# A fused sliding-window attention and channel mix: v in rows of two tokens, batch 0 by plain loads, bias products apart, new instruction orders

## The chip, the cores and the metric

One Trainium2 chip, of which the kernel uses one core. The time of a run is the device time of one launch in microseconds (us). Engines: TensorE (PE), VectorE (DVE), ScalarE (ACT), GpSimd (POOL) and SyncE (SP); in this kernel POOL and SP issue the DMA transfers.

## The reference

q, k and v are of the shape (8, 8, 576, 64), that is batch, heads, tokens, head size, in fp32. The attention has a sliding window of 128 tokens and an ALiBi bias; its result is the input of a channel mix.

```python
scores = (1.0 / np.sqrt(D)) * np.matmul(q, k.transpose(0, 1, 3, 2))
rel = pos[:, None] - pos[None, :]
slopes = 2.0 ** (-8.0 * (np.arange(H) + 1) / H)
bias = slopes[:, None, None] * (-np.abs(rel))[None]
mask = (rel >= 0) & (rel < 128)
attn = softmax(np.where(mask, scores + bias[None], -1e9))
x = np.matmul(attn, v)                     # (8, 8, 576, 64)
x = x.transpose(0, 2, 1, 3).reshape(8, 576, 512)
x_prev = x moved by one token, zeros first
xk = mu_k * x + (1.0 - mu_k) * x_prev
xr = mu_r * x + (1.0 - mu_r) * x_prev
k = np.maximum(xk @ w_k, 0.0)              # w_k 512 x 1024
out = 1.0 / (1.0 + np.exp(-(xr @ w_r))) * (k * k @ w_v)   # fp32, (8, 576, 512)
```

## The kernel before

The attention is cut into 32 items: item 4b + g is batch b with the head pair g (heads 2g and 2g + 1). The 576 tokens are four blocks of 128 and a tail of 64. Scores are made with keys on the partitions and queries along the free axis, so that the next product needs no transpose of them; of each block of keys only the 256 queries that can see it are computed, in two halves (`HALVES`) of 2 x 512 columns.

An item goes through these steps (in brackets the names of the steps in the order tables, then the tiles in the trace):

- Loads. v by POOL, cast to bf16 on the way, a block of 128 tokens at a time (lvs.b.j, tile vs; lvs.b.4 is the tail, tile tv). The vs and tv rows hold a column of ones beside each head, so that the product with v also gives the sum of the softmax. q and k of batches 1 to 4 by POOL, also cast, four tokens of a head to a partition row (lql, tile ql); batches 5 to 7 a block of tokens at a time (lqn, into the same tile) and then transposed by DMA from SP (tr, tile qt). The q and k of each batch's tail are loaded by POOL (lts, tile ts) and transposed on PE (tail, copied to tile tt by tcopy), or for batches 5 to 7 by DMA from SP (trt).
- In batches 0 to 4: a copy that puts tokens in order (ct on DVE, tile ct), transposes on PE (tq and tk, tile tp, line 166), copies out of PSUM (pq and pk, tile qk, line 146). For head pair 0 of batch 0, q and k come as fp32 by SP (lq, tile qt) and are cast by DVE (c, line 143).
- Scores (score.item.half, tile sa, line 229). Items 0 to 3 (`EARLY`) add the ALiBi bias and the mask on PE: a product of a scaled identity (sid) with a table of distances (dist) is summed into the same PSUM tile, line 206, in the same step. All later items instead multiply by a table after the exp.
- exp (exp, ACT, line 237, tile at), then that product by the table (mask, DVE, line 246; not for items 0 to 3).
- The product with v (av, PE, line 262), the division (norm, DVE, tile xu), the transpose to channels on the partitions (ot on PE and xt on ACT, or for items 12 and later a DMA transpose xt from SP), and the token shift (xk and xr, DVE; the tile dl is x minus its predecessor).

Pairs P of batches share one channel mix. Its columns are cut into chunks starting at c0: m1 (PE, line 326, w_k) gives one of 8 groups of 128 features, rl is its relu (ACT, line 332), kk the square (DVE line 341, or ACT line 338), m3 (PE, line 349, w_r) and rs (ACT tanh, line 355) the gate, m2a and m2 (PE, line 364, w_v) the two halves of the second product, oo its product with the gate (DVE, line 379), st the store (SP).

What runs when is written out by hand: a table `ORDER` gives for each engine the names of all its steps in a row, and `plan()` emits them in that order; each engine works through its row and waits where an input or a buffer isn't free. PSUM has two buffers for sa and four for everything else (mm). Before PE has anything to do it runs warm-up products on a zero tile (line 190; tile wm): eight written out, then `FILL` = (5, 2, 3).

Of the kernel before, what the change touches and what calls it, by code (L numbers as in the profile page):

```python
# [16 lines left out]
def kernel(  # L17
# [26 lines left out]
    W = D + 1  # L44
    NBUF = 4
# [31 lines left out]
    ldr = qt_buf[-1].rearrange("p i j g c -> p (i j g c)").bitcast(FP32)[  # L77
        :, 0:4 * NHW * NF * D].rearrange("p (i g h c) -> p i g h c", i=2, g=NHW, h=2)
# [32 lines left out]
    def load_qk(g, i):  # L111
        nc.sync.dma_start(
            out=ldr[:, i, g],
            in_=(q, k)[i][0, 2 * g:2 * g + 2, 0:SM].rearrange("h (p r) d -> p h (r d)", p=128))

    def load_v(b, j):
        if j < NF:
            nc.gpsimd.dma_start(  # L118
                out=vs_buf[b % NLD][:, j, :, 0:D],
                in_=v[b, :, 128 * j:128 * j + 128, :].rearrange("h p d -> p h d"))  # L120
        else:
            nc.gpsimd.dma_start(
                out=tv_buf[b % NLD][0:64, :, 0:D],
                in_=v[b, :, SM:S, :].rearrange("h p d -> p h d"))

    def load_qp(g, i):
        nc.gpsimd.dma_start(
            out=ql_buf[0][:, g // 2, i, 2 * (g % 2):2 * (g % 2) + 2],
            in_=(q, k)[i][0, 2 * g:2 * g + 2, 0:SM].rearrange("h (p r) d -> p h (r d)", p=128))
# [32 lines left out]
    def qk_transp(it, t0, t1):  # L162
        cs = T["cs", it]
# [19 lines left out]
    def tail_copy(b):  # L183
        t4 = T.pop(("tt", b))[:, 0:128 * G].rearrange("p (g t c) -> p g t c", g=G, t=2)
        nc.vector.tensor_copy(out=tt_buf[b % 2][:, :, 0:3:2], in_=t4)

    def warm(n):
        ps = p_mm.tile([128, 512], FP32, tag="mm", name="wm")
        for _ in range(n):
            nc.tensor.matmul(ps, lhsT=zero[:, 0:128], rhs=zero, start=True, stop=True)  # L190

    BASE = (0, 256, 512, 768, 960)
    HALVES = (((0, 0, 256), (1, 128, 256)),
              ((2, 256, 256), (3, 384, 128), (3, 512, 64), (4, 512, 64)))

    def scores(it, e):
# [4 lines left out]
        a0 = BASE[pieces[0][0]] + pieces[0][1] - 128 * pieces[0][0]  # L201
        w = sum(n for _, _, n in pieces)
        sa = T["sa", it, e] = p_sa.tile([128, 2, 512], FP32, tag="sa", name="sa")
        if early:
            for hl in range(2):
                nc.tensor.matmul(
                    sa[:, hl, 0:w] if e else sa[:, hl, 0:w].rearrange("p (u c) -> p u c", u=2),
                    lhsT=sid[:, 2 * g + hl],
                    rhs=dist if e else dist[:, None, 0:256].to_broadcast([128, 2, 256]),
                    start=True, stop=False, skip_group_check=True)  # L210
# [21 lines left out]
    def at_half(it, e):  # L232
        return at_buf[it % NAT][:, 0:2048].rearrange(
# [797 lines left out]
```

## Time and profile before

| what | value |
|---|---|
| runs | 231.13, 231.31, 230.84 us; median 231.13 us |
| profiled execution | span 230.5 us, 5326 instructions |
| PE matmul busy | 222.2 us, 96% of the span |
| DVE busy | 192.2 us, 83% |
| ACT busy | 155.4 us, 67% |
| POOL busy | 88.7 us, 38% |
| DMA | 33.56 MB read, 9.44 MB written, mean 146 GB/s of 16 engines' payload |

The span runs from the first to the last instruction of the profiled execution. Busy time of POOL and SP does not count the issue of a DMA as such; the lines of the trace named DMA_DIRECT2D on POOL are the work that POOL does to make a transfer's descriptors. In a line of the stretches, "10.00, 8.89 (x119)" after the window is its length, then busy time and instructions of PE, and so on for each engine in the order of the head line. In a line in order of time the first number is the start, the second the busy time of the group, and the bracket tells the idle time of the engine before it and what ended that. In a line of groups the bar separates names from busy time and mean (ns), and the last part is the idle time ahead of that group.

### The profile page before, as it was taken

The numbers are of one execution on the slowest core, as the hardware profiler recorded it, in microseconds if no ns is written. First come the engines' busy times: TensorE is split into PE (matmuls) and PEld (weight loads), VectorE is DVE, ScalarE is ACT, GpSimd is POOL, SyncE is SP. The second block draws the span as 40 slices with busy tenths as digits, with TensorE's granted clock in tenths as the row PEclk, the third lists the DMA queues.
The fourth block names the chain that finished last, engine by engine and source line by source line (L and its number), as shares of the span: only waits on it lengthen the run. The fifth ranks groups of instructions, "written<-read, shape, count | busy, mean of one in ns | idle before, by whom it ended". The sixth has DMA issues, their size and how long they took to land.

```text
span 230.5 us, 5326 instructions
## 1 busy us (share of the span) xinstructions
PE 222.2 (96%) x2099; PEld 130.0 (56%) x2099; DVE 192.2 (83%) x409; ACT 155.4 (67%) x265; POOL 88.7 (38%) x127
## 2 busy tenths in 40 slices
PE   7889899999999999999999999899999999999994
PEld 2446577855685565456657554455574555456653
DVE  7577999999998998999798996996876998985252
ACT  4299999985999998783789555685168744226700
POOL 8987857563897000697001954540000000000000
PEclk9999999999999999999999999999999999999999
DMA  6999999999999986999996999999954252413014
GB/s 137 160 173 187 198 177 192 195 180 162 177 155 161 154 120 100 123 128 204 120 256 144 166 120 156 203 176 197 134 128 119 79 163 77 102 46 141 0 67 162
DMA packets 117305, 33.65 MB, mean 146 GB/s; under 512 B 99608, under 2 KB 112928, under 8 KB 117280
## 3 DMA queue, kind: packets, MB, share of 16 engines
q0 software_dynamic: 83600, 16.52, 92.3%
q1 hardware_dynamic: 33680, 16.79, 34.1%
q8 instruction: 16, 0.26, 0.4%
q14 instruction: 9, 0.07, 0.1%
HBM read 33.56 MB, written 9.44 MB: 187 GB/s over the span
## 4 chain that ended last, share of the span: by engine, by line
PE 84%; ACT 7%; DMA 4%; DVE 2%; issue 1%; SPq 0%; DVEq 0%
PE pv L364 25%; PE ps L326 25%; PE pr L349 13%; PE sa L262 7%; PE sa L229 6%; DMA tt<-ts 4%; PE wm L190 3%; PE tp L166 3%; ACT at L237 3%; ACT qk L146 2%; PE pv L371 2%; ACT xt L287 1%; PE tp L282 1%; DVE qk L143 1%; ACT rl L332 1%
## 5 line engine op out<-in xcount | busy, mean ns | idle before, releaser
L237 ACT ACTIVATE at<-sa 128x1024 bf16<-128x1024 f32 x64 | 64.7, 1043 | 14.3 <-PE sa L229 14.2
L326 PE MATMUL ps<-xk,wk_sb 128*128 128x256 bf16 (+2 forms) x416 | 73.2, 314 | 0.5 <-DVE xk L315 0.4
L332 ACT ACTIVATE rl<-ps 128x256 bf16<-128x256 f32 (+2 forms) x104 | 46.3, 482 | 37.0 <-PE ps L326 30.0
L364 PE MATMUL pv<-wv_sb,kk 128*128 128x512 bf16 x272 | 65.3, 379 | 0.0
L326 PEld LDWEIGHTS <-wk_sb 128*128 128x128 bf16 x416 | 38.5, 98 | 24.1 <-issue 2.4
L364 PEld LDWEIGHTS <-kk 128*128 128x128 bf16 x272 | 25.5, 98 | 28.4 <-issue 1.3
L246 DVE TENSOR_TENSOR at<-at,mask 128x1024 bf16<-128x1024 bf16 x56 | 37.4, 684 | 1.9 <-ACT at L237 1.9
L118 POOL DMA_DIRECT2D vs<-in_v_dram x32 | 28.5, 897 | 26.3 <-PE sa L262 16.1
L341 DVE TENSOR_TENSOR kk<-rl 128x256 bf16<-128x256 bf16 (+2 forms) x88 | 28.0, 335 | 10.3 <-ACT rl L332 10.1
L349 PE MATMUL pr<-wr_sb,xr 128*128 128x512 bf16 x144 | 36.0, 379 | 0.0
L379 DVE SCALAR_TENSOR_TENSOR ot<-rs,pv 128x512 f32<-128x512 bf16 (+1 forms) x38 | 24.4, 653 | 7.4 <-PE pv L364 5.8
L315 DVE SCALAR_TENSOR_TENSOR xk<-dl,mu_sb,xt 128x576 bf16<-128x576 bf16 (+2 forms) x36 | 27.1, 752 | 1.3
L315 DVE SCALAR_TENSOR_TENSOR xr<-dl,mu_sb,xt 128x576 bf16<-128x576 bf16 x32 | 25.5, 812 | 0.0
L355 ACT ACTIVATE rs<-pr 128x512 bf16<-128x512 f32 x36 | 21.5, 608 | 4.9 <-PE pr L349 4.6
L262 PEld LDWEIGHTS <-at 128*128 128x128 bf16 x576 | 21.6, 98 | 5.3 <-issue 0.4
L274 DVE TENSOR_TENSOR xu<-sa,rc 128x640 bf16<-128x640 f32 x28 | 23.1, 824 | 1.2 <-DMA xt<-xu 0.3
L146 ACT COPY qk<-tp 128x1024 bf16<-128x1024 bf16 (+1 forms) x20 | 18.9, 960 | 5.6 <-PE tp L166 4.6
L349 PEld LDWEIGHTS <-xr 128*128 128x128 bf16 x144 | 13.2, 98 | 12.6 <-issue 0.4
L90 POOL DMA_DIRECT2D ql<-in_k_dram x12 | 10.9, 919 | 23.0 <-DVE ct L157 21.1
L262 PE MATMUL sa<-vs,at 128*128 128x65 bf16 x448 | 18.9, 194 | 0.0
L308 DVE TENSOR_TENSOR dl<-xt 128x576 bf16<-128x576 bf16 (+2 forms) x36 | 15.1, 420 | 3.2 <-DMA xt<-xu 2.1
L229 PE MATMUL sa<-qk 64*128 64x256 bf16 (+1 forms) x160 | 13.2, 259 | 0.8 <-ACT qk L146 0.5
(70 smaller groups left out, 207.6 us busy)
## 6 DMA issues: line engine op xcount, KB each, us to landing
out_dram<-ot SPq DMA_DIRECT2D x34, 256.0 KB, 3.6
vs<-in_v_dram POOLq DMA_DIRECT2D x32, 128.0 KB, 8.0
ql<-in_k_dram POOLq DMA_DIRECT2D x9, 256.0 KB, 6.7
ql<-in_q_dram POOLq DMA_DIRECT2D x9, 256.0 KB, 7.3
ql<-in_k_dram POOLq DMA_DIRECT2D x13, 128.0 KB, 6.5
ql<-in_q_dram POOLq DMA_DIRECT2D x13, 128.0 KB, 7.6
wk_sb<-in_moe_w_k_dram POOLq DMA_DIRECT2D x2, 512.0 KB, 9.0
wv_sb<-in_moe_w_v_dram POOLq DMA_DIRECT2D x2, 512.0 KB, 8.5
```

The lines of the kernel that those rows point to most:

```text
L118: nc.gpsimd.dma_start(out=vs_buf[b % NLD][:, j, :, 0:D], in_=v[b, :, 128 * j:128 * j + 128, :].rearrange("h p d -> p h d"))
L229: nc.tensor.matmul(to, lhsT=kk_, rhs=qq_, start=not early, stop=True, skip_group_check=True)
L237: nc.scalar.activation(out=at_half(it, e), in_=T.pop(("sa", it, e)), func=AF.Exp, scale=float(scale))
L246: nc.vector.tensor_tensor(out=at, in0=at, in1=m, op=ALU.mult)
L262: nc.tensor.matmul(pa[:, hl, W * (t - t0):W * (t - t0) + W], lhsT=at[:, lo:lo + 128], rhs=vs[:, u, 2 * g + hl, :] if u < NF else tvb[:, 2 ...
L315: nc.vector.scalar_tensor_tensor(out=to, in0=T["dl", it][:, c0:c1], scalar=mu_sb[:, NPO * which + g:NPO * which + g + 1], in1=xp, op0=ALU. ...
L326: nc.tensor.matmul(ps[:, 0:c1 - c0], lhsT=wk_sb[:, po, 128 * fo:128 * fo + 128], rhs=xk[:, po, c0:c1], start=(po == 0), stop=(po == NPO - 1))
L332: nc.scalar.activation(out=rl[:, 0:c1 - c0], in_=T.pop(("ps", P, c0, fo))[:, 0:c1 - c0], func=AF.Relu, scale=RELU_SCALE)
L341: nc.vector.tensor_tensor(out=T["kk", P, c0][:, fo, 0:c1 - c0], in0=rl[:, 0:c1 - c0], in1=rl[:, 0:c1 - c0], op=ALU.mult)
L349: nc.tensor.matmul(pr, lhsT=T["xr", P][:, po, 128 * c:128 * c + 128], rhs=wr_sb[:, po], start=(po == 0), stop=(po == NPO - 1))
L364: nc.tensor.matmul(pv, lhsT=kk[:, fo, o:o + 128], rhs=wv_sb[:, fo], start=(fo == 0), stop=(fo == NFO - 1))
L379: nc.vector.scalar_tensor_tensor(out=T["ot", P, c][:, w0:w1], in0=T["rs", P, c][:, w0:w1], scalar=1.0, in1=pv[:, 0:w1 - w0], op0=ALU.add, ...
```

## The change

What it does, part by part:

- *v.* `load_v` fetches rows of two tokens (2 x 64 numbers of a head) into partitions 0 to 63; a new step vc.b.z moves the odd tokens of two blocks to partitions 64 to 127, one copy for two blocks. On the partitions a block's tokens are then the 64 even ones and the 64 odd ones. k is brought into the same order: pk permutes in its copy, the lqn loads of k come in two halves of 64 partitions (36 loads for three batches, where there were 24), and dist and the mask are made for that order. The column of ones stands ahead of a head's numbers.
- *Batch 0.* All four head pairs come as fp32 through SP (8 loads, 2 before) into the two qt buffers, and are cast by steps c.g.i on three engines (2 on DVE, 4 on ACT, 2 on POOL) into the memory of ql; the four POOL loads of batch 0's q and k are gone, as are its three ct steps.
- *Bias.* The products with dist are steps of their own, bias.item.half, which can stand well ahead of the scores that add to them.
- *q and k copies.* pq and pk are steps of 512 columns each, for every item up to 19.
- *Tables.* dist and mask are 320 wide, not 512, and the copies that filled the rest (dcopy, mcopy) are gone; zero, dist, sid and the row of mu lie in the memory of w_v, so that the load of w_v waits for their last use.
- *Warm-ups.* `FILL` goes from (5, 2, 3) to (2, 2): 18 products become 12.
- *Squares.* 46 of 104 on ACT, where 16 were; 58 on DVE, where 88 were.
- *Other copies.* 4 of 16 xt copies go from ACT to DVE, two tcopy steps from DVE to ACT. 6 vc steps are on DVE, 10 on POOL. The ring of rs has 5 buffers instead of 6.
- *Orders.* All memsets stand ahead of POOL's first load, and all five tables are new.

The core of the diff:

```diff
-    vs_buf = [cst.tile([128, NF, H, W], BF16, name=f"vs{i}") for i in range(NLD)]
+    vs_buf = [cst.tile([128, NF, H, V0 + 2 * D], BF16, name=f"vs{i}") for i in range(NLD)]
...
     def load_v(b, j):
         if j < NF:
             nc.gpsimd.dma_start(
-                out=vs_buf[b % NLD][:, j, :, 0:D],
-                in_=v[b, :, 128 * j:128 * j + 128, :].rearrange("h p d -> p h d"))
+                out=vs_buf[b % NLD][0:64, j, :, V0:],
+                in_=v[b, :, 128 * j:128 * j + 128, :].rearrange("h (p r) d -> p h (r d)", r=2))
...
+    def v_copy(b, j, f):
+        vs = vs_buf[b % NLD][:, 2 * j:2 * j + 2].rearrange("p j h c -> p (j h) c")
+        f(vs[64:128, :, V0:V0 + D], vs[0:64, :, V0 + D:])
...
     def qk_copy(it, t0, t1, f):
         tp, o = (T["tp", it, t0], 0) if ("tp", it, t0) in T else (T["tp", it, 0], 512 * t0)
-        f(qk_buf[it % NBUF][:, t0:t1].rearrange("p t (c r) -> p t c r", r=NF),
-          tp[:, o:o + 512 * (t1 - t0)].rearrange("p (t r c) -> p t c r", t=t1 - t0, r=NF))
+        if t0:
+            f(qk_buf[it % NBUF][:, 1].rearrange("p (j e i w) -> p e j i w", j=NF, e=2, w=2),
+              tp[:, o:o + 512].rearrange("p (w e j i) -> p e j i w", w=2, e=2, j=NF))
+            return
+        f(qk_buf[it % NBUF][:, 0].rearrange("p (c r) -> p c r", r=NF),
+          tp[:, o:o + 512].rearrange("p (r c) -> p c r", r=NF))
...
+    def bias(it, e):
+        g = it % G
+        sa = T["sa", it, e] = p_sa.tile([128, 2, 512], FP32, tag="sa", name="sa")
+        for hl in range(2):
+            nc.tensor.matmul(
+                sa[:, hl].rearrange("p (u c) -> p u c", u=2),
+                lhsT=sid[:, 2 * g + hl],
+                rhs=both(dist, 0, 320, 1)[:, 0] if e else
+                dist[:, None, LT:].to_broadcast([128, 2, 256]),
+                start=True, stop=False, skip_group_check=True)
...
-    FILL = (5, 2, 3)
+    FILL = (2, 2)
...
+            if early:
+                op(("bias", it, h), "PE", 440, lambda h=h: bias(it, h), [("sid",)], n, "sa")
...
+                flex(("vc", b, z), "DVE", 600, lambda f, z=z: v_copy(b, z, f),
+                     [("lvs", b, 2 * z), ("lvs", b, 2 * z + 1)], 0)
...
         "POOL": """
-            lql.0.1.1 lql.0.1.0 clear0 lqp.1.1 lvs.0.0 lts.0.1 lqp.1.0 lts.0.0 lvs.0.1
+            clear0 ms clear lts.0.0 lts.0.1 lvs.0.0 lvs.0.1 lvs.0.3 lvs.0.2 c.2.0
+            lvs.0.4 lql.1.0.0 lql.1.0.1 lql.1.1.0 lts.1.0 c.3.0 vc.0.1 lts.1.1 lql.1.1.1
```

`flex` is `op` with the engine read from the table in which the step stands; `f` is then the copy of that engine (nc.vector.tensor_copy, nc.scalar.copy or nc.gpsimd.tensor_copy).

Three places in the rows. First POOL at the start, before: the end of the memsets of line 454 to 460 and the loads around the first loads of v (tile vs0) and of the tails (ts0); ql0 is q and k of batch 0.

```order
L403 IOTA dist_109 128x256
L138 DMA ql0_89<-in_k_dram 128x4x256
L138 DMA ql0_89<-in_q_dram 128x4x256
L454 MEMSET tv0_102 64x520
L455 MEMSET tv0_102 128x8
L456 MEMSET vs0_86 128x32
L460 MEMSET tt0_100 128x4x64
L127 DMA ql0_89<-in_k_dram 128x2x256
L118 DMA vs0_86<-in_v_dram 128x8x64
L132 DMA ts0_93<-in_k_dram 64x8x64
L127 DMA ql0_89<-in_q_dram 128x2x256
L132 DMA ts0_93<-in_q_dram 64x8x64
```

The same place after, from the last of the memsets on:

```order
L465 MEMSET tv2_104 64x528
L466 MEMSET tv2_104 128x8
L467 MEMSET vs2_88 128x32
L910 MEMSET tt1_101 128x4x64
L137 DMA ts0_93<-in_q_dram 64x8x64
L137 DMA ts0_93<-in_k_dram 64x8x64
L124 DMA vs0_86<-in_v_dram 64x8x128 x4
L154 CAST ql0_89<-qt1_92 128x2x4x64
L128 DMA tv0_102<-in_v_dram 64x8x64
```

Four loads of batch 0's q and k have left the row, all memsets have come to its front, and the four v loads of batch 0 stand together behind the two tail loads, with a cast behind them.

Second ACT at its start, before: the mask is made (line 428), and the first copies and exps of items.

```order
L428 ACT_TABLE_LOAD
L428 ACTIVATE mask<-dist 128x256 x4
L146 COPY qk_82<-tp 128x512
L237 ACTIVATE at_96<-sa 128x2x512
L146 COPY qk_84<-tp 128x512
L428 ACTIVATE mask<-dist 128x256 x2
L146 COPY qk_85<-tp 128x512
L237 ACTIVATE at_98<-sa 128x2x512
```

After (wv_sb is here the memory that holds dist):

```order
L443 ACT_TABLE_LOAD
L443 ACTIVATE mask<-wv_sb 128x320 x6
L151 CAST ql_89<-qt_91 128x2x4x64 x2
L443 ACTIVATE mask<-wv_sb 128x320 x2
L151 CAST ql_89<-qt_91 128x2x4x64
L151 COPY qk_82<-tp 128x512
L151 COPY qk_83<-tp 128x2x4x64
L262 ACTIVATE at_97<-sa 128x2x512
L262 ACTIVATE at_96<-sa 128x2x512
```

All eight mask steps now stand ahead of the first exp, three casts have come in, and the first exp has two copies ahead of it instead of one.

Third POOL late in the program, where the loads of batches 6 and 7 meet (buffers with the number 0 belong to batch 6 there, those with 1 to batch 7). Before:

```order
L118 DMA vs1_87<-in_v_dram 128x8x64
L132 DMA ts0_93<-in_q_dram 64x8x64
L132 DMA ts0_93<-in_k_dram 64x8x64
L118 DMA vs0_86<-in_v_dram 128x8x64 x2
L122 DMA tv0_102<-in_v_dram 64x8x64
```

After:

```order
L137 DMA ts0_93<-in_q_dram 64x8x64
L96 DMA ql1_90<-in_k_dram 64x8x64
L124 DMA vs0_86<-in_v_dram 64x8x128
L92 DMA ql0_89<-in_q_dram 128x8x64
L96 DMA ql0_89<-in_k_dram 64x8x64
L92 DMA ql0_89<-in_q_dram 128x8x64
L137 DMA ts0_93<-in_k_dram 64x8x64
L124 DMA vs1_87<-in_v_dram 64x8x128
```

Batch 6's tail loads (ts0) stood behind batch 7's first load of v (vs1), and now stand ahead of it.

More of the change, by code (lines that the diff above doesn't have):

```diff
@@ L200, in scores @@
         pieces = HALVES[e]
-        a0 = BASE[pieces[0][0]] + pieces[0][1] - 128 * pieces[0][0]
-        w = sum(n for _, _, n in pieces)
-        sa = T["sa", it, e] = p_sa.tile([128, 2, 512], FP32, tag="sa", name="sa")
+        a0 = 512 * e
         if early:
[L205 to L210, printed above, removed]
+            sa = T["sa", it, e]
+        else:
+            sa = T["sa", it, e] = p_sa.tile([128, 2, 512], FP32, tag="sa", name="sa")
         for (u, q0, n) in pieces:
@@ L427, in make_mask @@
         for h in heads:
-            nc.scalar.activation(out=mask[:, h, 0:256], in_=dist[:, 0:256],
+            nc.scalar.activation(out=mask[:, h], in_=dist,
                                  func=AF.Exp, scale=-(2.0 ** (-(h + 1))))
-    def copy_mask(i):
-        for (c0, n) in MSEG[i:i + 1]:
-            nc.vector.tensor_copy(out=mask[:, 0:H, c0:c0 + n], in_=mask[:, 0:H, 0:n])
     def load_wk(i):
@@ L478, in op, with flex @@
         return name
+    def flex(name, eng, busy, run, deps=(), pri=0, alloc=None, uses=()):
+        eng = ENGOF.get(name, eng)
+        f = {"ACT": act_cast, "DVE": vec_cast, "POOL": pool_cast}[eng]
+        return op(name, eng, busy, lambda: run(f), deps, pri, alloc, uses)
     def plan():
@@ L576, in add_pair @@
                    [("lts", 0, 0), ("lts", 0, 1)], n, "mm")
[L577 to L579 removed]
+                flex(("tcopy", 0), "DVE", 320, lambda f: tail_copy(0, f), [], n, uses=[("tail", 0)])
+            ready = [("pq", it), ("pk", it)]
+            vdep = []
         elif b in CROSSED:
@@ L906, in memsets_early @@
     def memsets_early():
-        for i in range(NAT):
-            nc.gpsimd.memset(at_buf[i][:, 2048:2112], 1.0)
         for i in range(2):
```

577 lines of the change are left out of this document (279 added, 298 removed).

## The prediction

> **What bounds the kernel now.** I read the page's parts 1 and 2 first, then the table of stretches, then the start in order of time, the groups by shape, and last the waits and the chain around the one hole that the table shows.
>
> ```profile
> PE 222.2 (96%) x2099; PEld 130.0 (56%) x2099; DVE 192.2 (83%) x409; ACT 155.4 (67%) x265; POOL 88.7 (38%) x127
> ...
> PE   7889899999999999999999999899999999999994
> ...
> DVE  7577999999998998999798996996876998985252
> ```
>
> PE is busy in 96% of the span, and its digits fall under 9 only in the first four or five slices, in one slice near 145 us and in the last. The stretches say the same in microseconds:
>
> ```profile
> core 0: us, PE busy (x) PEld busy (x) DVE busy (x) ACT busy (x) POOL busy (x), PEclk, DMA share, GB/s
> ...
> 10.00:20.00 10.00, 8.89 (x119) 5.28 (x120) 7.37 (x21) 9.05 (x17) 8.24 (x13) 1.00 1.91 167
> 20.00:30.00 10.00, 8.85 (x138) 6.45 (x135) 9.55 (x28) 10.00 (x16) 8.58 (x16) 1.00 1.37 201
> 30.00:40.00 10.00, 9.90 (x114) 7.36 (x112) 9.96 (x26) 9.81 (x21) 6.29 (x9) 1.00 1.80 182
> 40.00:50.00 10.00, 10.00 (x142) 7.06 (x140) 9.76 (x23) 9.43 (x16) 6.50 (x8) 1.00 1.55 192
> 50.00:60.00 10.00, 10.00 (x86) 5.59 (x85) 9.96 (x19) 6.57 (x11) 4.84 (x7) 1.00 2.29 185
> 60.00:80.00 20.00, 20.00 (x231) 13.21 (x230) 18.44 (x40) 18.89 (x34) 13.39 (x16) 1.00 1.80 144
> ...
> 140.00:160.00 20.00, 19.21 (x142) 9.65 (x141) 15.80 (x29) 13.67 (x24) 6.81 (x8) 1.00 2.06 185
> ```
>
> After 30 us PE loses nothing but 0.79 us in 140 to 160 and the tail. So the end is the end of the ramp plus a fixed amount of PE work: the change keeps every matmul except six warm-ups. Time can only come from the ramp or that hole, or go into a new wait. In the ramp ACT and DVE are the full ones: DVE idles 0.45, 0.04, 0.24 and 0.04 us in the four tens from 20 to 60, ACT 0.19 + 0.57 + 3.43 + 1.11 = 5.3 us from 30 to 80.
>
> **The ramp, step by step.**
>
> ```profile
> 0.74 1.28 ACT L428 ACT_TABLE_LOAD   x1 [0.74 <-PEq L1015]
> 0.84 0.34 POOL L403 IOTA dist<- 128x256 bf16 x1 [0.39 <-POOLq L1015]
> 1.19 6.44 PE L190 MATMUL wm<-zero 128*128 128x512 bf16 x16 [1.19 <-DVE zero L448]
> 2.63 1.33 ACT L428 ACTIVATE mask<-dist 128x256 bf16<-128x256 bf16 x4 [0.61 <-DVE dist L415]
> 3.03 0.53 POOL L454 MEMSET tv<- 64x520 bf16 x1
> 3.61 0.78 DVE L143 CAST cs<-qt 128x512 bf16<-128x512 f32 x1 [0.56 <-DMA qt<-in_q_dram]
> 4.05 0.70 POOL L127 DMA_DIRECT2D ql<-in_k_dram  x1
> 7.70 0.59 PE L190 MATMUL wm<-zero 128*128 128x512 bf16 x2
> 7.72 0.91 POOL L118 DMA_DIRECT2D vs<-in_v_dram  x1
> 7.90 0.59 ACT L146 COPY qk<-tp 128x512 bf16<-128x512 bf16 x1 [3.94 <-PE tp L166]
> 9.73 1.02 ACT L237 ACTIVATE at<-sa 128x1024 bf16<-128x1024 f32 x1 [1.25 <-PE sa L229]
> 11.56 0.59 ACT L146 COPY qk<-tp 128x512 bf16<-128x512 bf16 x1 [0.81 <-DVE qk L143]
> 14.30 0.53 PE L262 MATMUL pa<-vs,at 128*128 128x65 bf16 x12
> 16.34 1.93 ACT L237 ACTIVATE at<-sa 128x1024 bf16<-128x1024 f32 x2
> 19.88 0.65 POOL L454 MEMSET tv<- 64x520 bf16 x1
> 21.95 0.70 POOL L122 DMA_DIRECT2D tv<-in_v_dram  x1
> 28.75 0.49 ACT L332 ACTIVATE rl<-ps 128x256 bf16<-128x256 f32 x1
> ```
>
> ACT reaches its first relu at 28.75, the mark of a ramp that has ended. Before it ACT has idled 0.74 + 0.61 + 3.94 + 1.25 + 0.81 and loaded a table for 1.28, 8.6 us; the other 20.1 us are work. All five gaps lie before 11.56, where ACT waits for q and k. Prices of the work that moves:
>
> ```profile
> L146 ACT COPY qk<-tp 128x1024 bf16<-128x1024 bf16 x16 | 16.5, 1054 | 0.7 <-PE tp L166 0.7
> L157 DVE COPY ct<-ql 128x1024 bf16<-128x1024 bf16 x19 | 9.0, 481 | 0.1
> L146 ACT COPY qk<-tp 128x512 bf16<-128x512 bf16 x4 | 2.3, 584 | 4.9 <-PE tp L166 3.9 <-DVE qk L143 0.8
> L332 ACT ACTIVATE rl<-ps 128x256 bf16<-128x256 f32 x48 | 17.6, 415 | 7.4 <-PE ps L326 6.3 <-ACT at L237 0.6 <-DVE kk L341 0.4
> L338 ACT ACTIVATE kk<-rl 128x256 bf16<-128x256 bf16 x6 | 2.6, 426 | 0.0
> L287 ACT COPY xt<-tp 128x256 bf16<-128x256 bf16 x4 | 1.4, 394 | 0.0
> L341 DVE TENSOR_TENSOR kk<-rl 128x256 bf16<-128x256 bf16 x42 | 11.4, 284 | 2.5 <-ACT rl L332 2.4
> ```
>
> Neighbours on ACT overlap: two exps take 1.93, not 2 x 1.02, so I take 0.10 off each ACT mean.
>
> *ACT work up to the first relu.* Four fp32 casts are added, priced like the 128x512 copy, 0.48 each: +1.9. The q and k copies were four of 0.48 and three of 0.95 (4.8) and are ten of 0.48 (4.8): 0. Four of eight x copies go to DVE or behind the relu: 4 x 0.29 = -1.2. Eight masks are 320 columns wide instead of 256; by the relus of 256 and the copies of 512 above (0.17 for 256 columns) +0.05 each, +0.4. Exps stay eleven. Work: 20.1 + 1.1 = 21.2.
>
> *ACT idle.* Masks start when dist is ready: three more iotas (at most 0.34 each) and wider DVE steps, 2.63 becomes about 3.3. Then six masks (2.2), two casts, two masks and a cast end near 7.7, all on data that has come: the plain loads took 2.87 us (issue 0.74, cast at 3.61), and SP's tenth issue at its 0.5 us pace stands near 5. Transposes (0.4), copy, scores (0.4) put the first exp near 9.6; two copies fill half that wait, so 0.95 idle. Later the POOL cast of head pair 2 and the v copy cost perhaps 0.75. Idle 5.0; first relu at 21.2 + 5.0 = 26.2, that is 2.5 us earlier.
>
> *V.* POOL now does its memsets first: 1.02 (3.03 to 4.05) and 2.07 (19.88 to 21.95) come ahead of the first DMA, which moves from 1.34 to about 5.2. Four loads are gone from the front, so the second v load is issued near 7.2, against 7.72, into a queue with four fewer loads in it. Landing:
>
> ```profile
> DMA to landing us min/median/max: 3.8/8.0/14.7
> ```
>
> At 3.8 (the case of a short queue, which I take) v is there at 11.0, plus the copy of odd tokens on DVE (64x1024, like the ct copy 0.48): 11.5, against 14.30. At the 6.6 it took before (7.72 to 14.30) it is 14.3, and 2.5 us of ramp are gone again: the bound on the other side.
>
> *DVE.* It drops three ct copies (1.4), the dist and mask copies (about 1.5 with what surrounds them) and, over the kernel, 30 squares at 0.28 or more (about 9); it gains six v copies (2.9), four x copies and two q copies (about 3). DVE is the emptier by 6 us; it does not carry the new end.
>
> *What survives.* The kernel needs the same PE work from there, but ACT is fuller: up to the start of pair 1 it gets ten more squares (10 x 0.33 = 3.3), two tail copies (1.0) and loses one x copy (0.6), 3.7 of the 5.3 us that it idled. It fits with 1.6 to spare; with ACT so close to PE's pace I let 1.0 of the 2.5 go. Bounds: all of it kept, or all lost and up to 1 more. Term: -1.5.
>
> *Warm-ups.* 18 become 12. The first 16 took 0.40 each, the last two at 7.70 add 0.21 each: PE runs at half pace until about 7. The bias matmuls, now ahead of the q and k transposes, stand where the six were, so PE stays as busy: 0, between -0.4 and +1. The Trainium skill (TensorE: Matmul & The Clock Gate, "What's actually happening") says that the full clock comes after about 3.4 us of sustained work; the rows fit it roughly. Were PE's work in 5 to 10 us too thin for that, a few transposes would cost double, inside the same +1.
>
> **The hole at 145 us.**
>
> ```profile
> PE sa L229 <- DMA tt<-ts: 0.8, 1, 0.8
> 125.81 0.88 POOL L118 DMA_DIRECT2D vs<-in_v_dram  x1 [16.09 <-PE sa L262]
> 126.68 0.69 POOL L132 DMA_DIRECT2D ts<-in_q_dram  x1
> 137.48 8.18 DMA tt<-ts
> ```
>
> The scores of batch 6 wait for its tail transpose; its tail loads stood behind a v load of batch 7 that waited 16.09 us for batch 4's weighted sums. In the new POOL order the tail loads stand ahead of every load of batch 7's v, and SP's two tail transposes ahead of batch 6's q. Late next would be the q and k transposes, whose 24 loads are now 36; POOL is idle for 16 us there. Term: -0.8, between -0.8 and 0.
>
> *Loads in the steady part.* V rows of two tokens halve v's pieces; k by even and odd keys adds 12 issues of about 0.7 us on a POOL that is 38% busy. PE waited for no load but the one above: 0. The tail after the last matmul keeps its order of half products and stores: 0.
>
> *POOL copies.* Ten v copies and two casts now run on POOL. No row shows a POOL copy; the nearest is the memset, 0.53 for 520 columns, so 1024 take about 1.1, between 0.5 and 2.2. Beside DVE they cost between nothing and their whole length. I take 0.5 in all, since most lie behind 60 us, where DVE has gaps.
>
> **Sum.** Span 230.5 - 1.5 - 0.8 + 0.5 = 228.7. The median of the runs, 231.13, lies 0.6 above this span, so 229.3.
>
> **Rivals.**
> Slower, by one mechanism: POOL's copies hold DVE. Four of them (batch 1 and 2) fall into 24 to 64 us, where DVE had 0.5 us to spare; each holding one DVE operation for 1.1 gives 4.4: 228.7 - 0.5 + 4.4 less about 1 of new DVE room, 231.6, or 232.2 as a run. It decides from 0.8 us held per copy on. For it: DVE is nearly always in an operation with two inputs there. Against it: in this trace POOL's work beside DVE left DVE's means as they are, but that work only wrote. The Trainium skill (SBUF — State Buffer, "Who interferes with whom") says that a DVE instruction with two SBUF inputs and a GpSimd instruction that reads SBUF block each other whole; by it this rival is the rule, and no row here can test it. Chance 0.16.
>
> ACT becomes the bound: its 1.6 us of cover is used up by waits on casts and copies, the whole 2.5 is lost and 1 to 2 more: 230.5 + 1.5 - 0.8 + 0.6 = 231.8. Against it: 5.3 us stood idle. Chance 0.09.
>
> No change: v lands as late as before, the ramp stays, and the hole closes in part: 230.7 to 231.6. Chance 0.13.
>
> More than forecast: the ramp's 2.5 is kept whole and POOL costs nothing: 227.2, 227.8 as a run. Chance 0.15.
>
> **The numbers.** The forecast, 228.4 to 230.6, has 0.47. About 0.2% (0.46 us) is what a measurement of this kernel can tell from no change. Faster: 0.47 + 0.15 = 0.62; same 0.13; slower 0.16 + 0.09 = 0.25. From 227.4 to 232.2 some 0.1 is left out on each side: below, a ramp over 3 us shorter; above, both slow rivals together.
>
> **What the trace after would show.** First relu near 26; PE's first product with v near 12; no wait for tt near 145; ACT near 170 us busy; DVE near 185 with the mask's mean still 684 ns. Wrong if the mask's or the square's mean has grown (POOL holds DVE), if PE waits for relus between 30 and 80 (ACT is the bound), or if v lands after 13.

## The result, and the profile after

240.91 us, the median of four runs, against 231.01: slower, ratio 1.0414 (95% interval 1.0379 to 1.0449). The forecast was 229.3 us, range 227.4 to 232.2; no rival reached 240. A time below is the median of all runs of a kernel, while a ratio leaves out its slow runs, so a ratio can be lower than its median suggests.

First the page of the kernel after, its busy times, its slices and the clock:

```profile
PE 223.5 (93%) x2093; PEld 130.4 (54%) x2093; DVE 195.4 (82%) x382; ACT 167.6 (70%) x311; POOL 99.0 (41%) x146
...
PE   7699878996999986999999999999999999999994
...
DVE  6379999999899969989897999799695999555113
...
PEclk9799999999799999999999999999999999999999
```

PE works as long as before (223.5 us, 222.2 before), but in a span longer by 8.9 us; the slices 2, 6, 10 and 16 (6 us each, digits 6 and 7) hold holes that before does not have. The row of the clock, all nines before, has two sevens, around 9 and 63 us. The stretches put times on it (length, then PE, PEld, DVE, ACT and POOL busy, then the granted clock):

```profile
0.00:10.00 10.00, 6.49 (x26) 2.59 (x27) 5.21 (x18) 6.19 (x13) 8.89 (x27) 0.91 0.92 228
10.00:20.00 10.00, 9.49 (x127) 5.79 (x125) 7.27 (x22) 8.38 (x13) 9.94 (x15) 0.92 1.53 159
...
30.00:40.00 10.00, 7.95 (x108) 6.14 (x107) 9.76 (x20) 8.21 (x19) 8.66 (x11) 1.00 1.44 175
...
50.00:60.00 10.00, 7.99 (x75) 4.41 (x73) 9.89 (x15) 8.69 (x15) 8.03 (x11) 0.97 1.53 152
60.00:80.00 20.00, 19.74 (x232) 13.59 (x231) 18.86 (x38) 16.29 (x33) 14.61 (x21) 0.93 1.40 122
80.00:100.00 20.00, 16.80 (x185) 9.36 (x184) 17.45 (x30) 13.91 (x25) 11.47 (x15) 1.00 1.54 163
```

PE busy, with before's in brackets: 7.95 from 30 to 40 us (9.90), 7.99 from 50 to 60 (10.00), 16.80 from 80 to 100 (20.00), and at the start 6.49 (8.30). The clock falls below 1 behind the hole at the start and behind the one at 56 to 58 us, and stays at 1.00 around the other two; from 140 to 160 us, where before had its hole, PE is full. What PE waited for, total, number and longest:

```profile
PE sa L288 <- DVE at L272: 2.4, 2, 2.2
PE tp L174 <- ACT ql L151: 2.2, 1, 2.2
PE ps L340 <- DVE xk L329: 1.7, 1, 1.7
PE pv L378 <- DVE ot L393: 1.3, 2, 1.0
...
PE ps L340 <- ACT rl L346: 1.1, 1, 1.1
```

Three of the five lead to DVE (at, xk, ot), one to ACT's cast (ql) at the start, one to ACT's relu, and that relu (at 35.88 us) had itself waited 1.07 us for a square on DVE. DVE is as full as before in 20 to 60 us, and gets less done (83 operations, 96 before). The groups show it:

```profile
L272 DVE TENSOR_TENSOR at<-at,mask 128x1024 bf16<-128x1024 bf16 x56 | 39.7, 726 | 2.9 <-ACT at L262 2.9
...
L300 DVE TENSOR_TENSOR xu<-sa,rc 128x640 bf16<-128x640 f32 x28 | 23.1, 824 | 1.0
...
L355 DVE TENSOR_TENSOR kk<-rl 128x256 bf16<-128x256 bf16 x24 | 8.2, 349 | 4.8 <-ACT rl L346 4.8
```

The mask's mean is 726 ns (684 before), the square's of 256 columns 349 (284). The division of line 300, which reads PSUM, kept its 824 ns. One place, in order of time:

```profile
54.51 2.37 DVE L327 TENSOR_TENSOR dl<-xt 128x576 bf16<-128x576 bf16 x1
...
54.91 1.05 POOL L154 COPY vs<-vs 64x1024 bf16<-64x1024 bf16 x1
...
56.56 1.21 POOL L154 COPY vs<-vs 64x1024 bf16<-64x1024 bf16 x1
...
56.91 1.47 DVE L329 SCALAR_TENSOR_TENSOR xk<-dl,mu_sb,xt 128x576 bf16<-128x576 bf16 x1
...
58.44 0.49 PE L340 MATMUL ps<-xk,wk_sb 128*128 128x256 bf16 x3 [1.74 <-DVE xk L329]
```

A subtraction that takes 453 ns takes 2.37 us while a POOL copy of odd tokens runs; the next operation, 0.82 us elsewhere, takes 1.47 beside the second copy; PE waits 1.74 us for it. Of the ten POOL copies eight have a partner on DVE that takes longer than usual. Each partner's time less the usual one of its form: 1.55, 0.84, 1.92, 0.65, 0.32, 0.31, 1.24 and 0.78, in all 7.6 us of DVE. Seven of the partners read two inputs from SBUF; the fifth is a copy of v on DVE, with one input (0.74 us, 0.42 alone). POOL can pay too: one copy that met three masks at their usual 685 ns took 2.20 instead of 1.05. Who holds whom can't be read from the starts as recorded: three of the held operations (at 31.58, 54.51 and 90.16 us) start 0.3 to 0.6 us before their copy does.

The second cause is at the start:

```profile
3.80 1.28 ACT L443 ACT_TABLE_LOAD   x1 [3.80 <-DVE wv_sb L434]
...
5.09 2.27 ACT L443 ACTIVATE mask<-wv_sb 128x320 bf16<-128x320 bf16 x6
5.14 0.59 PE L219 MATMUL sa<-wv_sb 128*128 128x512 bf16 x2
...
7.26 1.12 ACT L151 CAST ql<-qt 128x512 bf16<-128x512 f32 x2
...
7.92 0.77 PE L174 MATMUL tp<-ident,ql 128*128 128x128 bf16 x8 [2.19 <-ACT ql L151]
...
8.48 1.06 PE L219 MATMUL sa<-wv_sb 128*128 128x512 bf16 x2
```

The table load of ACT, at 0.74 before, now waits for DVE's distances and starts at 3.80; the masks start at 5.09, the casts stand behind six of them, and PE, out of warm-ups, waits 2.19 us for a cast. After that hole the clock is low: the same two bias products took 0.59 at 5.14 and 1.06 at 8.48. The first exp and the first product with v:

```profile
11.99 1.94 ACT L262 ACTIVATE at<-sa 128x1024 bf16<-128x1024 f32 x2 [1.08 <-PE sa L254]
...
14.30 0.36 PE L288 MATMUL pa<-vs,at 128*128 128x65 bf16 x6
```

9.73 and 14.30 before. The third cause is on SP and DVE, at 80 to 92 us. SP, and then DVE and PE:

```profile
80.62 1.30 SPq L107 DMA_TRANSPOSE xt<-xu  x1
81.97 0.57 SPq L398 DMA_DIRECT2D out_dram<-ot  x1
...
83.97 5.30 SPq L398 DMA_DIRECT2D out_dram<-ot  x4
```

```profile
88.22 0.69 DVE L393 SCALAR_TENSOR_TENSOR ot<-rs,pv 128x512 f32<-128x512 bf16 x1 [2.11 <-DMA out_dram<-ot]
...
88.97 1.02 PE L378 MATMUL pv<-wv_sb,kk 128*128 128x512 bf16 x4 [1.04 <-DVE ot L393]
...
90.16 1.93 DVE L272 TENSOR_TENSOR at<-at,mask 128x1024 bf16<-128x1024 bf16 x1
...
92.15 0.63 PE L288 MATMUL sa<-vs,at 128*128 128x65 bf16 x15 [2.15 <-DVE at L272]
```

The store st.0.1, whose product was finished at 51.9 us (oo.0.1, the order table read against DVE's rows), stands on SP behind xt.15, a transpose of an item that is ready only at 80.6. Four output buffers are full until then; the fifth product waits 2.11 us for one, and PE waits 1.04 for it. The last two rows are a held mask again, with a hole of 2.15 us behind it.

### The profile page after: what moved, and what is told of

Read it like the earlier page. It is cut to its first block, busy times and chain, and to the rows that moved or that the text cites. A ratio compares the mean times of both kernels' runs of the same rounds, so it can differ in the third digit from the quotient of the medians.

```text
span 239.4 us, 5390 instructions
## 1 busy us (share of the span) xinstructions
PE 223.5 (93%) x2093; PEld 130.4 (54%) x2093; DVE 195.4 (82%) x382; ACT 167.6 (70%) x311; POOL 99.0 (41%) x146
## 4 chain that ended last, share of the span: by engine, by line
PE 68%; ACT 10%; POOL 7%; DVE 6%; DMA 5%; issue 2%; SPq 0%; POOLq 0%; ACTq 0%; DVEq 0%
PE pv L378 22%; PE ps L340 21%; PE pr L363 11%; PE sa L288 5%; PE sa L254 5%; ACT at L262 4%; DMA out_dram<-ot 3%; DMA ql<-in_q_dram 2%; DVE at L272 2%; ACT qk L151 2%; POOL vs L124 2%; PE tp L174 2%; PE pv L385 1%; ACT mask L443 1%; DVE kk L355 1%
## 5 line engine op out<-in xcount | busy, mean ns | idle before, releaser
L346 ACT ACTIVATE rl<-ps 128x256 bf16<-128x256 f32 (+2 forms) x104 | 47.8, 487 | 36.1 <-PE ps L340 26.3
L262 ACT ACTIVATE at<-sa 128x1024 bf16<-128x1024 f32 x64 | 65.9, 1052 | 7.2 <-PE sa L254 7.0
L378 PE MATMUL pv<-wv_sb,kk 128*128 128x512 bf16 x272 | 66.2, 384 | 1.3 <-DVE ot L393 1.3
L272 DVE TENSOR_TENSOR at<-at,mask 128x1024 bf16<-128x1024 bf16 x56 | 39.7, 726 | 2.9 <-ACT at L262 2.9
L393 DVE SCALAR_TENSOR_TENSOR ot<-rs,pv 128x512 f32<-128x512 bf16 (+1 forms) x38 | 24.5, 655 | 18.3 <-PE pv L378 9.7
L124 POOL DMA_DIRECT2D vs<-in_v_dram x32 | 22.7, 720 | 16.8 <-issue 12.2
L288 PEld LDWEIGHTS <-at 128*128 128x128 bf16 x576 | 21.6, 99 | 8.9 <-DVE at L272 3.7
L355 DVE TENSOR_TENSOR kk<-rl 128x256 bf16<-128x256 bf16 (+2 forms) x58 | 20.2, 368 | 7.1 <-ACT rl L346 6.9
L151 ACT COPY qk<-tp 128x512 bf16<-128x512 bf16 x34 | 19.6, 623 | 7.5 <-PE tp L174 6.1
L96 POOL DMA_DIRECT2D ql<-in_k_dram x24 | 16.8, 720 | 15.5 <-DMA qt<-ql 13.0
L352 ACT ACTIVATE kk<-rl 128x256 bf16<-128x256 bf16 (+2 forms) x46 | 21.9, 497 | 0.3
L327 DVE TENSOR_TENSOR dl<-xt 128x576 bf16<-128x576 bf16 (+2 forms) x36 | 17.0, 472 | 1.5 <-DMA xt<-xu 1.3
```

Source lines behind the costliest of these rows:

```text
L124: nc.gpsimd.dma_start(out=vs_buf[b % NLD][0:64, j, :, V0:], in_=v[b, :, 128 * j:128 * j + 128, :].rearrange("h (p r) d -> p h (r d)", r=2))
L151: nc.scalar.copy(out=dst, in_=src)
L262: nc.scalar.activation(out=at_half(it, e), in_=T.pop(("sa", it, e)), func=AF.Exp, scale=float(scale))
L272: nc.vector.tensor_tensor(out=at, in0=at, in1=m, op=ALU.mult)
L288: nc.tensor.matmul(pa[:, hl, W * (t - t0):W * (t - t0) + W], lhsT=at[:, lo:lo + 128], rhs=(vs[:, u, 2 * g + hl] if u < NF else tvb[:, 2 * ...
L346: nc.scalar.activation(out=rl[:, 0:c1 - c0], in_=T.pop(("ps", P, c0, fo))[:, 0:c1 - c0], func=AF.Relu, scale=RELU_SCALE)
```

## The experiments

Ratios are to the kernel before, run beside it. Moves in the order tables are shown as names.

**POOL copies by themselves.** Eight copies are put into the kernel *before*.

```diff
 "POOL": ... lts.2.1 +pc.0 ... lts.3.1 +pc.1 ... lql.3.1.1 +pc.2 ... lql.3.0.0 +pc.3
         ... lvs.2.3 +pc.4 ... lvs.2.2 +pc.5 ... lql.4.0.0 +pc.6 ... lql.4.1.0 +pc.7
+    for i in range(8):
+        op(("pc", i), "POOL", 1000,
+           lambda: nc.gpsimd.tensor_copy(out=junk[64:128], in_=mask[0:64, 0:2]), ...)
```

> The kernel before with eight POOL copies of 64x1024 put into POOL's row between 33 and 56 us, from the mask to a tile that nobody reads: the price of a POOL copy by itself, where DVE has less than 0.3 us to spare in ten. Theory A (holding): each copy holds a two-input DVE operation by 0.8 to 1.6 us, together 6 to 10 us; 235 to 240 us with PE idle between 35 and 65 us. Rival (POOL and DVE work side by side, as the prediction took for likely): 0 to 1 us, 231 to 232 us.

239.95 us, ratio 1.0395 (1.0367 to 1.0422): 9.0 us for eight copies. Theory A holds. The copies, two rows of DVE with their partners (two squares, 0.28 each alone; two masks, 0.68 each alone), and the stretches:

```profile
L986 POOL COPY junk<-mask x8: 1057/1158/2113, 33.5 to 56.1; 64x1024 bf16<-64x1024 bf16 x8
```

```profile
36.13 2.16 DVE L341 TENSOR_TENSOR kk<-rl 128x256 bf16<-128x256 bf16 x2
...
40.47 2.95 DVE L246 TENSOR_TENSOR at<-at,mask 128x1024 bf16<-128x1024 bf16 x2
```

```profile
30.00:40.00 10.00, 7.40 (x74) 5.24 (x71) 10.00 (x19) 6.92 (x15) 8.17 (x10) 1.00 1.79 179
40.00:50.00 10.00, 8.34 (x100) 5.36 (x101) 9.93 (x14) 6.58 (x11) 10.00 (x12) 0.83 1.51 185
50.00:60.00 10.00, 8.72 (x97) 5.02 (x95) 9.82 (x17) 7.23 (x10) 7.13 (x9) 1.00 2.58 145
```

The overlong DVE operations from 33 to 58 us add up to some 9.4 us over their usual times (0.2 in before), and the kernel lost 9.0: where DVE has nothing to spare, a held microsecond is about a lost one. PE is busy 24.5 of 30 us there (29.9 before), and after a hole of 3.1 us at 40 the clock of the ten falls to 0.83. PE waited for no load, so it is not that the copies hold up POOL's transfers. Not every overlong operation stands beside a copy in the record: a square at 38.81 us and the second mask (41.91) are 0.83 us too long beside POOL's descriptor work alone, and a ct at 48.85 is 1.06. As before has the same descriptor work and almost none of this in that stretch, the copies cause it, but by which step of POOL is open.

**The copies on DVE.** All ten, then all but the two of batch 7, then those two alone.

```diff
-"POOL": ... vc.0.1 ... vc.1.0 ... vc.1.1 ... vc.2.1 ... vc.2.0 ... vc.3.1 ... vc.4.0 ... vc.5.0 ... vc.7.0 ... vc.7.1
+"DVE": xt.1.0 vc.0.1 / xr.2 vc.1.0 / kk.0.0.4 vc.1.1 / xk.5 vc.2.1 / oo.0.2 vc.2.0 / vc.3.0 vc.3.1
+       norm.15 vc.4.0 / norm.12 vc.5.0 / xr.18 vc.7.0 / oo.1.6 vc.7.1
```

> The changed kernel with its ten POOL copies of odd tokens (vc) put on DVE, at the places in DVE's row that go with their times. Theory A (a POOL copy and a two-input DVE operation on SBUF hold each other): no DVE operation is longer than its own usual time beside a vc; the eight held ones lose their 7.6 us, ten copies of 0.42 us add 4.2 us; PE's holes at 33 to 36 and 56 to 60 us shrink, the granted clock stays at 1.00 from 58 to 64 us; 234 to 237 us, against 240.9. Theory B (ACT, with 30 more squares and the casts, is the bound): DVE's time doesn't matter, 240 to 242 us.

245.92 us, ratio 1.0676 (1.0602 to 1.0750): slower than with the copies on POOL, which neither theory had. The holds were gone: after 10 us no operation with two inputs is 0.1 us over its usual time. At 100 us this kernel was 5.5 us ahead of the changed one (the second transpose of batch 5's tail at 95.6 instead of 101.1 us), but then PE waited 4.4 us for q and k of batch 6 and 2.2 us more for a DVE that itself waited 7.2 us for transposes of x. So the last two copies were moved by themselves.

> The changed kernel with only the two POOL copies of batch 7 on DVE; the eight others stay on POOL. Theory (burst: POOL then runs through batch 7's loads without a stop): the loads from lvs.7.3 on are issued by about 145 us instead of 154, the transposes of batch 6 and of x beside them take 2 to 3 times as long, PE loses 6 to 10 us between 145 and 160 us; 246 to 250 us. Rival (the hole with all ten copies on DVE came from somewhere else): 240 to 241.5 us.

252.22 us, ratio 1.0930 (1.0880 to 1.0981). The theory of the burst holds, at more than the 246 to 250 us expected. SP's transposes in the changed kernel, and in this one, and PE's wait:

```profile
133.83 2.88 SPq L101 DMA_TRANSPOSE qt<-ql  x1
...
138.03 2.18 SPq L101 DMA_TRANSPOSE qt<-ql  x1
140.93 6.56 SPq L107 DMA_TRANSPOSE xt<-xu  x4
```

```profile
134.76 4.17 SPq L101 DMA_TRANSPOSE qt<-ql  x1
...
140.26 6.84 SPq L101 DMA_TRANSPOSE qt<-ql  x1
147.20 9.89 SPq L107 DMA_TRANSPOSE xt<-xu  x4
```

```profile
PE sa L254 <- DMA qt<-ql: 5.3, 1, 5.3
```

The two transposes of batch 6 went from 2.9 and 2.2 us to 4.2 and 6.8, the four of x from 6.6 to 9.9. In the changed kernel POOL stops twice at 132 to 144 us for landing v; without these copies it issued a dozen loads more in that time. DVE didn't wait for the v of the two copies that it now makes, so their place in its row is not the reason. The copies that held DVE also held back loads that nobody needed yet.

> Eight of the ten POOL copies (batches 0 to 5) go to DVE; the two of batch 7 stay on POOL. With all ten on DVE the kernel was 5.5 us ahead of the changed one from 95 to 135 us and lost over 10 us in a new hole at 145 us, where POOL, no longer waiting for batch 7's v, had issued all of batch 7's loads from 126 to 139 us beside the transposes of batch 6. Theory A (held DVE work, and a burst of loads that the two last copies keep apart): no hole at 145 us, the two transposes of batch 6's q and k take 3 and 2 us, 235 to 236 us. Rival (a copy on DVE is no better than one on POOL): 240 to 242 us.

237.73 us, ratio 1.0299 (1.0266 to 1.0332): no hole at 145 us (though the first of the two transposes took 5.2 us there, not 3), and 2.7 us less than the changed kernel by the ratios (1.0414 - 1.0299 of 231). That is less than the 5 to 6 expected. Eight copies of 0.42 us each, 3.4 us, are now DVE's own work; how much of them costs time no run settles.

**Loading v without copies.**

```diff
-                out=vs_buf[b % NLD][0:64, j, :, V0:],
-                in_=v[b, :, 128 * j:128 * j + 128, :].rearrange("h (p r) d -> p h (r d)", r=2))
+            for e in range(2):
+                    out=vs_buf[b % NLD][64 * e:64 * e + 64, j, :, V0:V0 + D],
+                    in_=v[b, :, 128 * j:128 * j + 128, :].rearrange("h (p r) d -> r p h d", r=2)[e])
```

> The changed kernel without any copy of odd tokens: each block of v is loaded in two halves of 64 partitions, even tokens and odd tokens, so 64 loads of v where there were 32, and no vc at all. Theory A (holding): all of the 7.6 us of held DVE time and the six DVE copies (2.5 us) are gone, 232 to 235 us, less than with the copies on DVE. Rival (loads are what matters): POOL issues 32 more loads of about 0.7 us and v lands later, 238 us or more, with PE waiting for v.

248.08 us, ratio 1.0725 (1.0690 to 1.0761). The rival's number, but not only by its mechanism: PE is busy only 12.87 of 20 us from 140 to 160, as in the run with all ten copies on DVE (13.06), with a wait of 5.0 for q and k of batch 6, and not for v; besides, PE waited 2.6 us for a ct at 40 us and 1.2 for a tail's load at 75.

**Stores first.**

```diff
-"SP": ... lq.3.1 xt.15 st.0.1 trt.5.1 st.0.3 st.0.0 st.0.2 st.0.4
+"SP": ... lq.3.1 st.0.1 st.0.0 st.0.2 st.0.3 xt.15 trt.5.1 st.0.4
```

> The changed kernel with the stores st.0.0 to st.0.3 ahead of xt.15 on SP, nothing else. Theory (SP's row: four finished products wait for a late transpose, and the fifth finds no buffer): DVE's wait of 2.1 us for a store at 88 us and PE's hole of 1.0 us there are gone; 239 to 240 us. Rival (the hole is only passed on to the held mask behind it): 240.5 to 241 us, with a longer wait for DVE's mask at 90 us.

238.25 us, ratio 1.0318 (1.0251 to 1.0385), 2.2 us less by the ratios, more than expected; DVE's wait of 2.1 us for a store is gone (the longest left is 0.9). Part of it is luck: with the new times the copy at 90 us met a square that it held 0.13 us, where it had held a mask 1.24, and all holds together come to 6.4 us instead of 7.6.

> The run before with st.0.0 to st.0.3 ahead of xt.15 on SP as well. Theory (both causes add, since one is held DVE time and the other a wait for an output buffer at 84 us): 233 to 234.5 us. Rival (the store's wait only hides what the copies cost): as without it, 235 to 236 us.

236.83 us, ratio 1.0255 (1.0216 to 1.0294). With the copies on DVE the stores are worth 1.0 us, but the interval overlaps that of the run without them (1.0266 to 1.0332), so neither the gain nor whether the two causes add in full is settled.

**The start.**

```diff
+    nc.scalar.activation(out=warmed, in_=zero[0:1, 0:2], func=AF.Exp)
     make_dist()
```

> The changed kernel with one tiny exp on ACT ahead of everything, so that the table load stands at 0.7 us and doesn't wait for the distances. Theory (the table load of 1.28 us behind its new wait delays the casts and so the first transposes): masks start near 3.7 instead of 5.1 us, the transposes that wait for ACT's cast at 7.9 us start near 6.6, PE's hole of 2.2 us is 0.9, first exp near 10.7; 239.5 us. Rival (lost again in the full stretch from 20 to 60 us): first exp earlier, time the same, 240.5 to 241 us.

241.91 us, ratio 1.0394 (1.0355 to 1.0433, from two runs of 239.5 and 240.6 us): no gain that can be measured, though the masks start at 3.82, the first exp at 9.91 and the first relu at 27.49 (28.27 in the changed kernel). Some of what comes early is lost again: the copies hold DVE for 8.6 us in all instead of 7.6, and PE waits 0.9 us for w_k at 28 us. On the kernel with eight copies on DVE and the stores first, with warm-ups (the result is the repaired kernel below):

```diff
-    FILL = (2, 2)
+    FILL = (6, 2)
```

> The kernel with eight copies on DVE and the stores first, with the table load early and four warm-up products more (FILL (6, 2)). Theory C (the ramp's term failed because ACT starts late and PE falls idle at 6 to 8 us, after which it is granted little over half its clock until 12 us): clock 1.00 in every stretch, first exp near 9.9, first relu 2 us earlier than the 29.1 us without it; 235 us against 236.8. Rival (DVE and ACT are full from 20 to 90 us, an earlier start is lost in them): 236.5 to 237 us, with a longer DVE wait somewhere after 20 us or more PE gaps there.

234.82 us, ratio 1.0152 (1.0115 to 1.0188), 2.4 us less by the ratios. Theory C holds in its main points: the clock is 1.00 in every stretch to 200 us, and PE's hole at 6 to 8 us is gone. But the first relu comes at 28.17, 1.0 us earlier than without it (29.14) and not 2, and the run doesn't part the early table from the warm-ups. Stretches, and what PE still waits for:

```profile
0.00:10.00 10.00, 8.79 (x44) 3.71 (x44) 5.45 (x19) 7.11 (x16) 8.89 (x28) 1.00 0.93 232
10.00:20.00 10.00, 7.84 (x114) 4.91 (x110) 7.42 (x22) 8.30 (x12) 9.21 (x14) 1.00 1.51 157
...
30.00:40.00 10.00, 9.14 (x118) 7.15 (x118) 9.63 (x23) 9.36 (x22) 7.19 (x10) 1.00 1.35 176
...
80.00:100.00 20.00, 18.87 (x186) 10.03 (x188) 18.69 (x36) 15.46 (x24) 3.70 (x5) 1.00 1.04 127
```

```profile
PE sa L288 <- DVE at L272: 1.2, 3, 0.6
...
PE sa L254 <- ACT qk L151: 0.9, 1, 0.9
PE to L191 <- DMA ts<-in_k_dram: 0.9, 1, 0.9
...
PE tp L174 <- DVE ct L165: 0.5, 1, 0.5
```

**Copies by DMA.**

```diff
-"DVE": ... vc.0.0 ... vc.0.1 ... vc.1.0 ... vc.1.1 ... vc.2.1 ... vc.2.0
+"SP": ... lq.3.1 vc.0.0 vc.0.1 vc.1.0 vc.1.1 st.0.1 st.0.0 vc.2.1 vc.2.0 st.0.2 ...
```

> The kernel with eight copies on DVE and the stores first, with the six copies of batches 0 to 2 taken off DVE and made by DMA from SP. Theory D (DVE is the bound from 20 to 90 us, so the copies of v cost there what they last, 6 x 0.42 = 2.5 us): 234 to 235 us, against 236.8. Rival (the time went into ACT and the start, not into DVE): 236.5 us or more; a DMA of 1024 pieces of 128 bytes may also land late, with PE waiting for vs at 15 or 37 us.

249.84 us, ratio 1.0805 (1.0753 to 1.0857). The doubt at the end of the expectation was right:

```profile
vs<-vs SPq DMA_DIRECT2D x6, 128.0 KB, 8.4
```

8.4 us to landing (last column); PE waited 5.5 us up to 20 us and 6.0 up to 70 for such a copy. It tells nothing on DVE.

> Both of the two runs before together: copies of batches 0 to 2 by DMA, early table, four warm-ups more. If both theories hold they add: 232 to 233.5 us. If the start only feeds full engines: as with the DMA copies alone.

251.18 us, ratio 1.0852 (1.0810 to 1.0894). PE waited 8.5 us at its first product with v (the profile puts it down to a tail load) and 6.3 us for such copies; nothing follows on the start.

**The hole of before.**

```diff
-"POOL": ... lvs.5.3 lvs.7.1 lts.6.0 lts.6.1 lvs.6.0
+"POOL": ... lvs.5.3 lts.6.0 lts.6.1 lvs.7.1 lvs.6.0
```

> The kernel before with batch 6's two tail loads moved ahead of batch 7's first load of v on POOL, and nothing else: the prediction's term for the hole at 145 us by itself. Theory (the term was right): no wait for tt, 0.8 us less, ratio 0.9965, 230.2 us. Rival (something else is late there at once): ratio 1.000, with another wait of PE near 145 us.

232.11 us, ratio 1.0016 (0.9986 to 1.0045). PE's wait for tt is gone from the profile, but no time is gained that these runs could show; the forecast ratio, 0.9965, lies outside the interval. In the profile nothing else is late there (PE is busy 19.89 us from 140 to 160, 19.21 before), and its span is 229.0 us against 230.5, some 0.5 of it from the start. But that execution was one of the shortest of its kernel; why the others were longer stays open.

**What is left.** The repaired kernel (234.8) still lies 1.5% above before. Three variants of it:

```diff
+        if b in (3, 4, 5):
+            return          # in v_copy
```

> The kernel with eight copies on DVE, stores first and repaired start (234.8 us), with the six copies of batches 3, 4 and 5 left out altogether, so that half of their v is old: only the time is read. Theory D (DVE is the bound up to 100 us and a copy costs there what it lasts): four of the six lie between 70 and 95 us, 4 x 0.42 = 1.7 us less, 233 us. Rival (PE's small gaps have another cause): 234.5 to 235 us.

233.91 us, ratio 1.0105 (1.0065 to 1.0146).

```diff
-"ACT": kk.0.256.5 kk.0.256.7 kk.0.0.7 kk.0.256.3 kk.0.256.2
+"DVE": kk.0.256.1 kk.0.256.5 / xr.0 kk.0.256.7 kk.0.0.7 / norm.6 kk.0.256.3 / ct.11 kk.0.256.2
```

> The kernel with eight copies on DVE, stores first and repaired start (234.8 us), with five of pair 0's first squares moved from ACT back to DVE (0.28 each there, 0.42 on ACT). Theory D (DVE is the bound from 30 to 60 us): 5 x 0.28 = 1.4 us more, 236 us. Theory E (ACT is the bound there): up to 5 x 0.33 = 1.6 us less, 233 us. If neither: 234.8 us.

235.69 us, ratio 1.0192 (1.0161 to 1.0223).

```diff
+        if j < NF and b in (3, 4, 5, 6):
+            for e in range(2): ...      # two loads of 64 partitions, no vc
```

> The kernel with eight copies on DVE, stores first and repaired start (234.8 us), with v of batches 3 to 6 loaded in two halves of 64 partitions and their eight copies gone; 16 loads more on POOL, which waits some 13 us between 93 and 107 us. Theory D: as with the copies left out, 233 us or a little less. Rival (loads): the 11 us more of issues make the loads of batches 4 and 5 late, PE waits for v or for q and k between 70 and 150 us, 235 us or more.

235.25 us, ratio 1.0174 (1.0134 to 1.0215).

The first leaves six copies out (and so computes with old values): less work on DVE went with less time (-1.1 us by the ratios, 1.7 expected), and from 80 to 100 us, behind four of the six (70 to 77 us) and around a fifth (87), PE is busy 19.78 us instead of 18.87. The second has more work on DVE and took more time (+0.9, 1.4 expected). Both go the way of theory D (DVE is the bound up to 100 us) and against theory E (ACT). The third has eight copies fewer on DVE and no gain (+0.5): the rival's number, 235 or more. In its profile PE gets the same 80 to 100 us back (19.85), but waits 2.0 us for w_k at 28 to 30 us, with a clock of 0.84 in the ten behind it, and 1.1 for a tail load at 74. That is its longest execution, and the others show a clock of 1.00, so where they lost the gain stays open. The intervals of all three overlap that of the 234.8 us kernel, so this is a direction, not a proof. None of the variants beats before.

## Why the prediction was wrong

*The step that failed most is the term for POOL's copies.* It took 0.5 us in all, on the ground that most lie where DVE has gaps and that no row of before showed a price. Only five of the ten lie behind 60 us, and DVE was busy 17.5 to 18.9 of 20 us there. The copy's length was estimated well (1.1, 1.05 measured), but the sum took the price at the low end of its range. Put into the kernel before, eight of them cost 9.0 us, 1.1 each; in the changed kernel they held DVE for 7.6 us, and moving eight of them to DVE gave back 2.7, with 3.4 us of their work then on DVE. The rival that ended slower had the mechanism and the place (24 to 64 us), and its 4.4 us for four copies is near the 5.0 that these four held; it gave 232.2 because it left out the later copies (two of them held a mask and a mix by 1.24 and 0.78), the clock, the start and the stores, and kept the ramp's 1.5 as won. The argument against it, that POOL's work had left DVE's means as they are, held for the operations with two inputs alone: in before a ct beside POOL's work took 0.80 us at 9.32, 0.42 usually. The rule weighed there, of the Trainium skill (SBUF — State Buffer, "Who interferes with whom"), that a DVE instruction with two SBUF inputs and a GpSimd instruction that reads SBUF block each other whole and that the first to issue wins, is in its first half what the trace shows: masks, squares, subtractions and mixes were held, the division from PSUM was not, and a copy that met three masks took 2.20. The second half no run here shows, as recorded starts don't go with it. The chance of 0.16 was too low for a rule that speaks of a whole block.

*The ramp, -1.5 forecast.* First relu at 28.27 instead of 26.2, against 28.75 before. ACT's idle was the mis-sized part: its work was 21.6 us (21.2 forecast), its idle with the table load 6.7 (5.0). Dist ready at 3.3 was nearly right (3.7), but the table load was taken as staying at 0.74; it started at 3.80, behind DVE's distances, and the masks at 5.09 instead of 3.3. V landed at 12.66, against 11.0 forecast (POOL issued that load at 8.07 instead of 7.2, and it took 4.6 instead of 3.8 us), its copy was made at 13.59, when DVE was free, and the first product with v began at 14.30, as late as before. (In before that load had landed at 13.43; the 14.30 that the forecast read as its landing is the start of the product.) And the price of PE's hole at 6 to 8 us was not the idle alone: "0, between -0.4 and +1" for the six warm-ups became 2.4 us by the repair, which changes the late table and four warm-ups together.

*What survives of the ramp* was argued from ACT's 5.3 idle us. That DVE "does not carry the new end" was probably a wrong step: from 10 to 100 us it makes eleven copies of v (5.2 us in the repaired kernel), and the longest sum of PE's waits behind the start is for DVE (at 1.2, xu 0.8, ct 0.5); but ACT (qk 0.9 and 0.5, at 0.6) is not far behind, and no run decides between them.

*SP.* The forecast named SP's tail transposes and missed that st.0.1 had moved behind xt.15 in SP's row: 2.2 us alone, of which part is luck, and 1.0 beside the other repair, within the noise.

*The hole at 145 us* closed as forecast: no wait for tt. Its 0.8 us could not be found again in before by itself.

*Busy times.* ACT 167.6 us (170 forecast) was right. DVE was 195.4 against 185; 7.6 of the difference is held time.

So of the 9.6 us that the ratio gives, the repairs together took back 6.1 (1.0414 to 1.0152): some 3.7 by copies and stores together, 2.4 by the start. The cause of the other 3.5 stays open, and so does that of the forecast gain of 1.7 us, which no variant showed; the last runs point to DVE.

## What to carry to other kernels

An operation moved to an idle engine is priced by what it does to the engines beside it, not by the room on its own: look at what the full engine is doing at that time, and if that has two SBUF inputs, count the whole length of a POOL copy as lost. Read every queue's row past each step that moves, SP's too, and read the waits of the first instruction on each engine. And before taking a wait off an issuing engine ask which transfers it had been keeping apart.

## What the runs showed of the hardware

- A POOL copy of 64x1024 bf16 takes 1.05 us, and took 2.2 beside three masks of DVE; an operation of DVE with two inputs from SBUF was held by 0.31 to 1.92 us beside such copies, a copy with one input by 0.32, a division from PSUM not at all.
- Holes of PE of 1.7 to 3.1 us were followed in two kernels by a lower clock (in the kernel after 0.86, 0.50 and 0.79 in the two-microsecond stretches from 58 to 64 us, behind the hole that ends at 58.4: 3.4 us at half pace, if it is half or full); one of 2.15 us at 90 us was not, in the same run. So a hole can cost more than its length, and not always does.
- A DMA of 1024 pieces of 128 bytes within SBUF landed 8.4 us after its issue (median of six).
- DMA transposes from SP that took 2.2 and 6.6 us took 6.8 and 9.9 beside a burst of loads.
